# Fewer unsplit units, a gate on ScalarE alone, and stores from places of their own, in an attention and feed-forward kernel

## The chip, the cores and the metric

The kernel runs on one core of one Trainium2 chip. The metric is the device time of one execution in microseconds (us). TensorE's matmuls are called PE in the profile and its weight loads PEld; VectorE is DVE, ScalarE is ACT, GpSimd is POOL, and SyncE (SP) issues nearly all DMAs. A difference of about 0.5% is what a measurement of this kernel can tell from no change.

## The reference

Two attention steps come first and a feed-forward layer after them, for 8 batches of 576 tokens with 8 heads of 64:

```python
def sm_attn(qq, kk, vv):
    s = scale * np.matmul(qq, kk.transpose(0, 1, 3, 2))
    s = s - np.max(s, axis=-1, keepdims=True)
    a = np.exp(s)
    a = a / (np.sum(a, axis=-1, keepdims=True) + 1e-09)
    return np.matmul(a, vv)
p_packed = sm_attn(p, k, v)              # 32 packed queries over 576 keys
out = sm_attn(q, p_packed, p_packed)     # 576 queries over 32 packed keys
# x: out with its heads joined, 4608 x 512
h = x @ w_in                             # 512 -> 2048
g = h * (1.0 / (1.0 + np.exp(-1.702 * h)))
return g @ w_out                         # 2048 -> 512
```

## The kernel before

All data is fp32. A large product takes each operand as two fp32r parts, an upper part (the operand cast) and a lower part (what the cast left), and three matmuls: upper by upper, upper by lower, lower by upper. The cast is `g_upper`, `h_upper` and so on (a CAST by ScalarE at line 178 or by VectorE at line 180), the rest `g_lower` or `h_lower` (a subtraction by VectorE or GpSimd).

**Batch 0** is computed in a way of its own, while the weights still arrive: per block f of 128 hidden units and per part of the tokens, `h_mm` makes h in one of two PSUM banks (h_72 and h_73 in traces), `h_tanh` (line 729, ScalarE) takes tanh(1.702 h) from the bank, `h_gate` (line 706, VectorE) makes (tanh + 1) * h with the bank read once more, and `out_mm` (line 763) multiplies by w_out. For the exponential of the softmax (`exp1`, `exp2`) and tanh, one table of ScalarE serves; `Gelu_apprx_sigmoid` needs another table, and a switch is an ACT_TABLE_LOAD.

**Batches 1 to 7** run in rounds n = 2 to 15, two a batch, of 288 tokens each; 256 of them are worked on at once and the other 32 (the rest) are kept in DRAM until a round of their own ("over", 0) or ("over", 1) works on the rests of four batches. A round has 8 units p, one for each pair of hidden blocks. For a unit, `hp_mm` makes h of both blocks in the one two-bank PSUM tile `hh` (line 713), `hp_gelu` (line 820, ScalarE) writes the gated values to SBUF, to one of two places that take turns, and `hp_over` (line 827, a DMA that SyncE issues) stores the rest to DRAM out of that place. The next `hp_mm` can begin when `hp_gelu` has read `hh`.

The output product of a unit comes in two kinds. A unit of the set `PLAIN` is unsplit: four `plain` steps of three matmuls with 512 columns each. Any other unit is split by Winograd's scheme into seven `product` steps of three matmuls with 256 columns each. For a split unit, sums of the gated values are needed (`sums_1`, `sums_2`, `sums_3`, lines 839, 843 and 847, by VectorE or GpSimd) and the sums' upper and lower parts too (a second `g_upper` and `g_lower`), and w_out's sums are made once (`conv_1` to `conv_4`). Both kinds add up in four PSUM banks (acc_63 to acc_66 are acc[0] to acc[3]); after a round `take_1` to `take_6` join them and `keep` (line 930) stores them.

One table named `order`, written out in the kernel, holds some 3,500 steps. Each engine executes its part of the table in the table's order. An instruction that waits holds up everything behind it on its engine, and a DMA that waits for its data holds up all later DMAs of SyncE, the loads of q, k, v (`load`) and of kept weights (`win_in`, line 308) among them.

## Time and profile before

| | |
|---|---|
| median of 3 runs | 680.41 us (677.87, 680.41, 680.8) |
| profiled execution | 675.16 us |
| span of its instructions | 673.4 us |
| TensorE busy | 659.1 us, 98% of the span |
| VectorE, ScalarE, GpSimd busy | 76%, 51%, 30% of the span |
| granted TensorE clock, mean | 0.999 |

The profiled execution is one execution of its own, 0.8% under the median of the runs; 1.8 us of its time lie outside the span. "Busy" of TensorE says little about its pace, since matmuls are pipelined and their ends are modelled; starts of neighbouring matmuls tell its pace better.

### The profile page before, as it was taken

What the parts mean: (1) busy time and instruction counts of PE and PEld (TensorE: products, weight loads), DVE (VectorE), ACT (ScalarE), POOL (GpSimd) and SP (SyncE); (2) the same over time, 40 slices, a digit from 0 to 9 for tenths busy, and PEclk for the clock granted to TensorE, in tenths of its full rate; (3) what the DMA queues carried; (4) which work ended last, traced back from release to release, by engine and by line L of the source; (5) the groups of instructions that cost most, each with busy time, mean ns of one, the idle gap of its engine ahead of it and who ended that gap; (6) DMA issues with size and microseconds to landing.
All of it is one profiled execution on the core that took longest, in us unless ns stands there. A gap on an engine that the chain in (4) does not pass through costs nothing. (4 is left out here: it accounts for less than half of the span.)

```text
span 673.4 us, 15533 instructions
## 1 busy us (share of the span) xinstructions
PE 659.1 (98%) x6037; PEld 591.1 (88%) x6037; DVE 510.9 (76%) x1123; ACT 340.8 (51%) x625; POOL 201.2 (30%) x238
## 2 busy tenths in 40 slices
PE   8999999999999999999999999999999999999997
PEld 6578777897889988998899998899979998899996
DVE  4999885786988788856977558786779667856486
ACT  4887647344673557633646535662446346432332
POOL 2531123413222333223334331321434233342320
PEclk9999999999999999999999999999999999999999
DMA  8998665226535453545643536462456435210132
GB/s 339 416 373 280 220 238 189 51 68 203 172 66 158 128 163 132 132 126 177 216 142 96 125 94 188 144 198 61 129 156 199 117 95 185 70 40 9 42 110 81
DMA packets 94250, 103.10 MB, mean 153 GB/s; under 512 B 69153, under 2 KB 74209, under 8 KB 89569
## 3 DMA queue, kind: packets, MB, share of 16 engines
q1 hardware_dynamic: 94016, 101.86, 49.0%
q8 instruction: 47, 0.77, 0.5%
q10 hardware_dynamic: 160, 0.26, 0.1%
q14 instruction: 27, 0.21, 0.1%
HBM read 80.14 MB, written 21.95 MB: 152 GB/s over the span
## 5 line engine op out<-in xcount | busy, mean ns | idle before, releaser
L876 PE MATMUL acc<-at_float32r 128*128 128x256 f32 (+1 forms) x2553 | 356.8, 290 | 0.1
L876 PEld LDWEIGHTS acc<-at_float32r 128*128 128x128 f32 x2553 | 327.5, 188 | 26.8 <-issue 14.2
L713 PE MATMUL hh<-at_float32r 128*128 128x288 f32 x1344 | 207.5, 297 | 1.4 <-ACT at_float L820 0.6
L713 PEld LDWEIGHTS hh<-at_float32r 128*128 128x128 f32 x1344 | 186.0, 188 | 7.9 <-ACT at_float L820 3.1
L820 ACT ACTIVATE at_float<-hh 128x576 f32<-128x576 f32 x112 | 73.0, 652 | 173.4 <-PE hh L713 113.5
L854 DVE TENSOR_TENSOR at_float32r<-at_float,at_float32r 128x416 fp32r<-128x416 f32 (+3 forms) x188 | 124.8, 674 | 30.9 <-ACT at_float32r L178 25.7
L178 ACT CAST at_float32r<-at_float 128x416 fp32r<-128x416 f32 (+7 forms) x171 | 93.9, 561 | 79.3 <-PE acc L876 44.7
L180 DVE CAST at_float32r<-at_float 128x512 fp32r<-128x512 f32 (+5 forms) x154 | 65.6, 430 | 43.6 <-PE acc L876 29.3
L854 POOL TENSOR_TENSOR at_float32r<-at_float,at_float32r 128x512 fp32r<-128x512 f32 (+3 forms) x53 | 66.0, 1248 | 109.3 <-DVE at_float32r L180 64.8
L839 POOL TENSOR_TENSOR at_float<-at_float 128x256 f32<-128x256 f32 x34 | 26.7, 785 | 89.3 <-DVE at_float32r L854 39.5
L763 PE MATMUL acc<-at_float32r 128*128 128x512 f32 x192 | 50.2, 396 | 0.0
L612 DVE TENSOR_TENSOR at_float32r<-b,at_float32r 128x512 fp32r<-128x512 f32 (+1 forms) x64 | 42.3, 674 | 6.2 <-ACT at_float32r L178 5.9
L843 POOL TENSOR_TENSOR at_float<-at_float 128x128 f32<-128x128 f32 x42 | 21.3, 509 | 79.6 <-DVE at_float L839 61.8
L839 DVE TENSOR_TENSOR at_float<-at_float 128x256 f32<-128x256 f32 x79 | 35.5, 452 | 12.4 <-ACT at_float L820 9.5
L763 PEld LDWEIGHTS acc<-at_float32r 128*128 128x128 f32 x192 | 34.2, 188 | 9.1 <-issue 2.1
L178 ACT CAST at_float32r<-b 128x512 fp32r<-128x512 f32 (+1 forms) x52 | 28.7, 579 | 21.4 <-PE b L597 19.1
L187 ACT ACT_TABLE_LOAD x29 | 37.2, 1283 | 0.5
L597 PE MATMUL b<-at_float,at_float 64*32 64x512 f32 (+1 forms) x512 | 33.9, 586 | 0.0
L713 PEld LDWEIGHTS h<-at_float32r 128*128 128x128 f32 x192 | 27.7, 189 | 6.9 <-DVE at_float L706 1.2
L713 PE MATMUL h<-at_float32r 128*128 128x320 f32 (+1 forms) x192 | 31.1, 301 | 1.0 <-DVE at_float32r L612 0.4
L843 DVE TENSOR_TENSOR at_float<-at_float 128x128 f32<-128x128 f32 x71 | 22.8, 325 | 11.3 <-POOL at_float L839 10.4
L847 POOL TENSOR_TENSOR at_float<-at_float 128x128 f32<-128x128 f32 x36 | 19.9, 554 | 35.2 <-DVE at_float L843 26.6
(127 smaller groups left out, 560.2 us busy)
## 6 DMA issues: line engine op xcount, KB each, us to landing
at_float<-w_kept SPq DMA_DIRECT2D x24, 1024.0 KB, 5.5
at_float<-v SPq DMA_DIRECT2D x8, 1024.0 KB, 6.0
o<-at_float SPq DMA_DIRECT2D x32, 256.0 KB, 3.3
at_float<-w_out SPq DMA_DIRECT2D x16, 511.8 KB, 5.3
at_float<-q SPq DMA_DIRECT2D x14, 576.0 KB, 5.1
at_float<-w_in SPq DMA_DIRECT2D x12, 511.8 KB, 7.6
at_float<-k_last SPq DMA_DIRECT2D x8, 640.0 KB, 5.2
at_float<-pk SPq DMA_DIRECT2D x8, 576.0 KB, 5.1
```

The costliest lines, as they stand in the source:

```text
L178: nc.scalar.copy(dst, src)
L180: engine.tensor_copy(dst, src)
L187: nc.scalar.activation(small("table", 1), ident[:, :1], func)
L597: nc.tensor.matmul(banks[eo][32 * j : 32 * j + 32, columns(part)], pt(b)[rows(eo), j, :], w[rows(eo), j, columns(part)], start=True, stop= ...
L612: nc.vector.tensor_tensor(lo, t[:, at], hi.bitcast(F32), op=ALU.subtract)
L713: nc.tensor.matmul(t[:, : halves(b)[half]], m_part(fc, eo, mp)[:, fo : fo + P], a_part(b, half, ap, eo), start=(n == 0), stop=(n == len(te ...
L763: nc.tensor.matmul(acc[i], g0(f, gp)[:, i * P : (i + 1) * P], wo(f, wp), start=(start and n == 0), stop=(stop and n == 2),)
L820: nc.scalar.activation(g, h, AF.Gelu_apprx_sigmoid, scale=2.0)
L839: engine.tensor_tensor(dst, src, by, op=ALU.subtract)
L843: engine.tensor_tensor(g_raw(n, p, 6), g_raw(n, p, 5), g_raw(n, p, 1), op=ALU.add)
L854: engine.tensor_tensor(lo, src, g_range(n, p, 0, which)[0].bitcast(F32), op=ALU.subtract)
L876: nc.tensor.matmul(acc[i][:, at : at + m], lhs, rhs, start=(start and k == 0), stop=(stop and k == len(pairs) - 1),)
```

## The change

Four things change, and the order table is written anew for them.

1. `PLAIN` has 8 units instead of 15: units (2, 5), (3, 3), (3, 4), (4, 0), (4, 1), (4, 2) and (5, 0) are now split. The steps `plain` go from 60 to 32, `product` from 791 to 840, and `sums_1`, `sums_2`, `sums_3`, `g_upper`, `g_lower` get 7 more each.
2. In batch 0, blocks 0 to 3 keep `h_tanh` and `h_gate`; blocks 4 to 15 use `h_gelu`, one ScalarE instruction in place of the two (24 of 32). It uses the table of `hp_gelu`.
3. A new step `rest` copies the 32-token rests of a unit (128 x 64 values) to a place of their own, one of two that take turns by the unit's parity, and `hp_over` stores from there. There are 112 such copies, 59 on ScalarE and 53 on GpSimd.
4. In the last round, ("over", 1), the values loaded back from DRAM get six places instead of two.

```diff
-    PLAIN = {(2, 0), (2, 1), (2, 2), (2, 3), (2, 4), (2, 5), (3, 0), (3, 1), (3, 2), (3, 3), (3, 4), (4, 0), (4, 1), (4, 2), (5, 0)}
+    PLAIN = {(2, 0), (2, 1), (2, 2), (2, 3), (2, 4), (3, 0), (3, 1), (3, 2)}
...
+    def h_gelu(b, f, half):
+        nc.scalar.activation(
+            th0(f, half), st["h", f, half][:, : halves(0)[half]], AF.Gelu_apprx_sigmoid, scale=2.0
+        )
...
     def g_words(n, p, at, m):
         i = G_INDEX[n, p]
-        return words((SPARE if i == 1 else DEC + i % 2 * G_RAW) + at, m)
+        if n == ROUNDS[-1]:
+            home = (DEC, DEC + G_RAW, KQ[0], KQ[0] + 8 * P, KQ[1], KQ[1] + 8 * P)[i % 6]
+        else:
+            home = SPARE if i == 1 else DEC + i % 2 * G_RAW
+        return words(home + at, m)
...
+    def aside(n, p):
+        at = X[2 + p % 2] + S
+        return words(at, 2 * HALF_REST).rearrange("p (j r) -> p j r", j=2)
+
+    def rest(n, p, engine=nc.scalar):
+        move(engine, aside(n, p), hp_view(n, p)[0][:, :, :HALF_REST])
+
     def hp_over(n, p):
         b = n // 2
-        g = hp_view(n, p)[0][:, :, :HALF_REST]
         r = slice(n % 2 * HALF_REST, (n % 2 + 1) * HALF_REST)
         dst = over_kept[b // 4][p].rearrange("p (j t) b r -> p j t b r", t=2)
-        nc.sync.dma_start(dst[:, :, b % 4 // 2, b % 2, r], g)
+        nc.sync.dma_start(dst[:, :, b % 4 // 2, b % 2, r], aside(n, p))
...
-        (scores1_copy, 1, 1, 1, act), (h_gate, 0, 0, 1), (load_w, 18), (out_mm, 0, 0, 0),
+        (scores1_copy, 1, 1, 1, act), (h_gate, 0, 0, 1), (load_w, 19), (out_mm, 0, 0, 0),
```

What the new table does is shown at three places. The first is SyncE around the two loads of q for batch 6 (L236; the rows named "over" are stores of rests, "o" are stores of results, "w_kept" and "pk" are loads of weights and of batch 7's k). Before:

```order
L827 DMA over_95<-at_float_350 256x1x32 x2
L236 DMA at_float_104<-q 128x1152
L827 DMA over_95<-at_float_350 256x1x32
L228 DMA at_float_104<-pk 128x1152
L827 DMA over_95<-at_float_350 256x1x32
L308 DMA at_float_107<-w_kept 128x2048
L236 DMA at_float_104<-q 128x1152
L930 DMA o<-at_float_1391 128x512 x2
```

And of the change:

```order
L842 DMA over_95<-at_float_250 256x1x32
L236 DMA at_float_104<-q 128x1152
L945 DMA o<-at_float_1384 128x512
L236 DMA at_float_104<-q 128x1152
L945 DMA o<-at_float_1384 128x512
L842 DMA over_95<-at_float_272 256x1x32
L842 DMA over_95<-at_float_250 256x1x32
```

Before, the first q load is the one for the first half of the scores, and the second half's comes behind two loads of other things. Now the second half's load is issued first, a store of results of round 10 stands behind it, and the first half's load behind that store.

The second place is ScalarE in batch 0, where the exponentials of batch 1's second softmax (L666) stand among the gates of blocks 11 to 15. Before:

```order
L729 ACTIVATE at_float_350<-h_72 128x320
L178 CAST at_float32r<-at_float_350 128x512
L666 ACTIVATE at_float_133<-at_float_133 128x576
L178 COPY at_float_481<-at_float_350 128x64
L729 ACTIVATE at_float_350<-h_73 128x256
L178 CAST at_float32r<-at_float_350 128x256
L729 ACTIVATE at_float_350<-h_72 128x256
```

And of the change, where L736 is `h_gelu` and L187 the small activation that calls for a table:

```order
L736 ACTIVATE at_float_350<-h_72 128x256
L187 ACT_TABLE_LOAD
L187 ACTIVATE at_float_89<-at_float_74 128x1
L666 ACTIVATE at_float_145<-at_float_145 128x576
L178 CAST at_float32r<-at_float_350 128x256
L178 COPY at_float_483<-at_float_350 128x64
L666 ACTIVATE at_float_133<-at_float_133 128x576
L736 ACT_TABLE_LOAD
L736 ACTIVATE at_float_350<-h_73 128x256
```

The exponentials now stand between two table loads, and no gate stands between them. Over the whole kernel the table loads go from 54 to 52.

The third place is the end of VectorE's program, the takes of the last round. Before:

```order
L903 TENSOR_TENSOR at_float_350<-acc_63,at_float_1391 128x256
L906 TENSOR_TENSOR at_float_1391<-acc_64,at_float_350 128x512
L924 TENSOR_TENSOR at_float_1391<-acc_66,at_float_1391 128x256
L913 TENSOR_TENSOR at_float_1391<-acc_64,at_float_1391 128x256
L919 TENSOR_TENSOR at_float_1391<-acc_65,at_float_1391 128x512
```

And of the change:

```order
L918 TENSOR_TENSOR at_float_350<-acc_63,at_float_1384 128x256
L921 TENSOR_TENSOR at_float_1384<-acc_64,at_float_350 128x512
L928 TENSOR_TENSOR at_float_1384<-acc_64,at_float_1384 128x256
L939 TENSOR_TENSOR at_float_1384<-acc_66,at_float_1384 128x256
L934 TENSOR_TENSOR at_float_1384<-acc_65,at_float_1384 128x512
```

Two of the takes have changed places. In the table, TensorE has six `product` steps left after the last one that adds to acc[0] before the change, and eight with it.

## Rows read from the trace of the kernel before

**Rows 1.** The page's head: the span, and each engine's busy time with its share of the span and its count of instructions.

```profile
span 673.4 us, 15533 instructions
PE 659.1 (98%) x6037; PEld 591.1 (88%) x6037; DVE 510.9 (76%) x1123; ACT 340.8 (51%) x625; POOL 201.2 (30%) x238
```

**Rows 2.** Who TensorE's matmuls waited for over the whole span: us in total, times, longest us. Rows of the first 25 us are left out.

```profile
PE hh L631 <- DMA at_float<-q: 1.6, 1, 1.6
...
PE hh L631 <- ACT at_float L820: 0.8, 2, 0.5
PE hh L631 <- ACT at_float L178: 0.7, 1, 0.7
...
PE hh L713 <- ACT at_float L820: 0.6, 2, 0.4
...
PE hh L713 <- ACT at_float L178: 0.4, 2, 0.3
...
PE h L713 <- DVE at_float L706: 0.3, 1, 0.3
```

**Rows 3.** TensorE's timeline in a stretch of 512-column matmuls (L763, and L876 as `plain`): start in us, us, instruction, count.

```profile
115.37 0.84 PE L763 MATMUL acc<-at_float32r 128*128 128x512 f32 x3
116.05 1.56 PE L876 MATMUL acc<-at_float32r 128*128 128x512 f32 x6
117.45 0.85 PE L763 MATMUL acc<-at_float32r 128*128 128x512 f32 x3
118.14 0.42 PE L713 MATMUL hh<-at_float32r 128*128 128x288 f32 x2
```

**Rows 4.** TensorE's timeline at the end of the program, 256-column matmuls (`product`) alone.

```profile
638.98 29.39 PE L876 MATMUL acc<-at_float32r 128*128 128x256 f32 x246
```

**Rows 5.** Groups of instructions by line and shape over the whole span: count, busy us, mean ns of one, idle time before them. L706 is `h_gate`, L839, L843 and L847 the three sums (L843 is shown for both engines), L854 `g_lower`, L178 a cast or copy of ScalarE.

```profile
L854 DVE TENSOR_TENSOR at_float32r<-at_float,at_float32r 128x512 fp32r<-128x512 f32 x87 | 62.3, 717 | 12.6 <-ACT at_float32r L178 9.6 <-PE acc L876 0.2
...
L178 ACT CAST at_float32r<-at_float 128x512 fp32r<-128x512 f32 x61 | 37.6, 620 | 35.5 <-PE acc L876 20.8 <-DVE at_float L847 10.0 <-POOL at_float L847 3.8
...
L839 DVE TENSOR_TENSOR at_float<-at_float 128x256 f32<-128x256 f32 x79 | 35.5, 452 | 12.4 <-ACT at_float L820 9.5 <-DMA at_float<-over 1.6 <-POOL at_float32r L854 0.4
...
L843 POOL TENSOR_TENSOR at_float<-at_float 128x128 f32<-128x128 f32 x42 | 21.3, 509 | 79.6 <-DVE at_float L839 61.8 <-DVE at_float L456 9.8 <-ACT at_float32r L178 7.4
...
L843 DVE TENSOR_TENSOR at_float<-at_float 128x128 f32<-128x128 f32 x71 | 22.8, 325 | 11.3 <-POOL at_float L839 10.4
L847 DVE TENSOR_TENSOR at_float<-at_float 128x128 f32<-128x128 f32 x77 | 22.6, 296 | 6.4 <-POOL at_float L843 5.8
...
L706 DVE SCALAR_TENSOR_TENSOR at_float<-at_float,h 128x320 f32<-128x320 f32 x16 | 7.5, 481 | 1.1 <-ACT at_float L729 0.7
...
L706 DVE SCALAR_TENSOR_TENSOR at_float<-at_float,h 128x256 f32<-128x256 f32 x16 | 6.6, 412 | 1.2 <-ACT at_float L729 1.1
...
L178 ACT COPY at_float<-at_float 128x64 f32<-128x64 f32 x7 | 1.7, 246 | 0.0
```

**Rows 6.** The timelines of SyncE and of TensorE around batch 6's q loads (L236), with what TensorE waited for in brackets; the last row is the time from issue to landing of the load issued at 483.59.

```profile
475.29 0.36 SPq L236 DMA_DIRECT2D at_float<-q  x1
...
481.93 0.36 SPq L228 DMA_DIRECT2D at_float<-pk  x1
...
483.02 0.53 SPq L308 DMA_DIRECT2D at_float<-w_kept  x1
483.59 0.43 SPq L236 DMA_DIRECT2D at_float<-q  x1
...
492.99 0.72 PE L631 MATMUL hh<-at_float,at_float 64*32 64x288 f32 x16 [1.56 <-DMA at_float<-q]
...
DMA to landing us min/median/max: 9.3/9.3/9.3
```

**Rows 7.** SyncE's timeline at batch 2's q loads, the second half's issued first, and the time to landing of the one issued at 152.00.

```profile
149.81 0.56 SPq L236 DMA_DIRECT2D at_float<-q  x1
...
152.00 0.60 SPq L236 DMA_DIRECT2D at_float<-q  x1
...
DMA to landing us min/median/max: 4.9/4.9/4.9
```

**Rows 8.** The chain that ended last, its end: start us, us, what (L913 is `take_4`, L919 `take_5`).

```profile
668.41 0.34 DVE at_float L913
...
668.84 0.69 DVE at_float L919
```

**Rows 9.** ScalarE's timeline at a table switch among the later rounds: a load, and the gate that needs the table.

```profile
229.16 1.28 ACT L820 ACT_TABLE_LOAD   x1 [0.47 <-issue]
230.46 0.65 ACT L820 ACTIVATE at_float<-hh 128x576 f32<-128x576 f32 x1
```

**Rows 10.** The timelines of GpSimd and VectorE where their instructions overlap, and the durations in ns of all of VectorE's first sums (min/median/max, first and last start in us).

```profile
567.10 1.17 POOL L676 TENSOR_TENSOR at_float<-at_float,at_float 128x576 f32<-128x576 f32 x1
...
567.18 1.37 DVE L839 TENSOR_TENSOR at_float<-at_float 128x256 f32<-128x256 f32 x1 [0.43 <-POOL at_float32r L854]
...
L839 DVE TENSOR_TENSOR at_float<-at_float x79: 361/424/1370, 135.0 to 662.8; 128x256 f32<-128x256 f32 x79
```

**Rows 11.** Of ScalarE's waits (us in total, times, longest us) the one for stores of rests, and of the DMA issues those stores (count, KB each, median us to landing).

```profile
ACT at_float L820 <- DMA over<-at_float: 8.0, 3, 4.2
...
over<-at_float SPq DMA_DIRECT2D x112, 32.0 KB, 2.3
```

More of the change, by code (lines that the diff above doesn't have):

```diff
@@ new lines @@
+        (conv_whole, 3, 0, dve), (product, 2, 7, 7), (hp_mm, 3, 2, 1), (g_lower, 3, 0, 0, dve),
+        (g_upper, 3, 1, 0, act), (conv_1, 3, pool), (take_1, 2), (hp_mm, 3, 2, 0), (take_2, 2),
+        (g_lower, 3, 1, 0, pool), (take_3, 2), (hp_gelu, 3, 2), (pack, 2, (6, 7)), (take_4, 2),
+        (rest, 3, 2, pool), (take_6, 2), (pack_end, 2), (load, 'q', 2, 1), (hp_mm, 3, 3, 0),
+        (take_5, 2), (hp_over, 3, 2), (hp_mm, 3, 3, 1), (conv_2, 3), (load, 'q', 2, 0),
+        (conv_3, 3, dve), (hp_over, 3, 1), (pack_turn_mm, 2, 6), (conv_4, 3, pool),
@@ new lines @@
+        (sums_3, 5, 1, pool), (take_3, 4), (hp_mm, 5, 3, 0), (g_lower, 5, 1, 0, dve), (take_4, 4),
+        (take_6, 4), (hp_gelu, 5, 3), (pack, 3, (6, 7)), (g_upper, 5, 1, 1, dve),
+        (g_lower, 5, 1, 1, dve), (take_5, 4), (sums_1, 5, 3, pool), (pack_end, 3),
+        (load, 'q', 3, 0), (product, 5, 0, 5), (hp_mm, 5, 4, 1), (rest, 5, 3, act),
+        (rest, 5, 2, pool), (hp_over, 5, 3), (sums_2, 5, 3, dve), (sums_1, 5, 2, dve),
+        (product, 5, 0, 1), (hp_over, 5, 2), (pack_turn_mm, 3, 6), (product, 5, 0, 4),
@@ new lines @@
+        (g_upper, 7, 0, 0, act), (rest, 7, 1, pool), (g_upper, 7, 1, 0, act),
+        (g_lower, 7, 0, 0, dve), (product, 6, 7, 5), (hp_mm, 7, 2, 1), (take_2, 6), (take_3, 6),
+        (hp_gelu, 7, 2), (sums_2, 7, 1, dve), (pack, 4, (6, 7)), (sums_3, 7, 1, dve), (take_4, 6),
+        (take_6, 6), (g_lower, 7, 1, 0, dve), (pack_end, 4), (load, 'q', 4, 0), (hp_mm, 7, 3, 1),
+        (hp_over, 7, 0), (take_5, 6), (hp_mm, 7, 3, 0), (hp_over, 7, 1), (g_upper, 7, 0, 1, dve),
+        (g_lower, 7, 0, 1, dve), (keep, 6, 1), (pack_turn_mm, 4, 6), (product, 7, 0, 4),
@@ new lines @@
+        (hp_mm, 9, 2, 1), (sums_3, 9, 1, pool), (take_1, 8), (g_upper, 9, 1, 0, dve),
+        (rest, 9, 0, act), (g_lower, 9, 0, 1, dve), (hp_over, 9, 0), (product, 8, 7, 7),
+        (hp_gelu, 9, 2), (product, 8, 7, 5), (g_lower, 9, 1, 0, dve), (product, 8, 7, 3),
+        (take_2, 8), (hp_mm, 9, 3, 0), (g_upper, 9, 1, 1, act), (take_3, 8), (hp_mm, 9, 3, 1),
+        (take_4, 8), (rest, 9, 2, pool), (take_6, 8), (hp_over, 9, 2), (take_5, 8),
+        (hp_gelu, 9, 3), (pack, 5, (6, 7)), (g_lower, 9, 1, 1, dve), (sums_1, 9, 3, pool),
@@ new lines @@
+        (rest, 10, 1, act), (product, 9, 7, 7), (turn1_blocks, 6, 0), (g_upper, 10, 1, 0, act),
+        (sums_3, 10, 1, pool), (product, 9, 7, 5), (m_upper, 5, 3, 1, None, act),
+        (g_lower, 10, 1, 0, pool), (hp_mm, 10, 3, 0), (turn1_out, 6, 0, 0), (take_3, 9),
+        (product, 9, 7, 3), (hp_over, 10, 2), (take_6, 9), (product, 10, 0, 1), (take_4, 9),
+        (g_upper, 10, 1, 1, act), (load, 'v', 6, 1), (product, 10, 1, 1), (take_5, 9),
+        (hp_over, 10, 1), (product, 10, 0, 6), (g_lower, 10, 1, 1, pool), (m_lower, 5, 3, 1),
@@ new lines @@
+        (hp_gelu, 11, 2), (take_4, 10), (pack, 6, (6, 7)), (g_lower, 11, 1, 0, dve),
+        (g_upper, 11, 0, 1, act), (g_upper, 11, 1, 1, dve), (g_lower, 11, 0, 1, dve),
+        (pack_end, 6), (load, 'q', 6, 1), (hp_mm, 11, 3, 1), (take_6, 10), (rest, 11, 2, act),
+        (take_5, 10), (product, 11, 0, 6), (keep, 10, 0), (product, 11, 0, 4), (load, 'q', 6, 0),
+        (g_lower, 11, 1, 1, dve), (product, 11, 1, 4), (keep, 10, 1), (product, 11, 0, 1),
+        (sums_1, 11, 2, dve), (hp_over, 11, 1), (hp_mm, 11, 3, 0), (sums_2, 11, 2, pool),
@@ new lines @@
+        (take_4, 13), (hp_mm, 14, 3, 1), (sums_3, 14, 2, dve), (keep, 13, 0),
+        (g_lower, 14, 1, 1, pool), (take_5, 13), (product, 14, 0, 7), (hp_gelu, 14, 3),
+        (product, 14, 0, 5), (product, 14, 0, 2), (m_upper, 7, 3, 0, None, act),
+        (sums_1, 14, 3, pool), (product, 14, 1, 2), (rest, 14, 3, act), (m_lower, 7, 3, 0),
+        (product, 14, 0, 1), (hp_over, 14, 3), (product, 14, 1, 7), (keep, 13, 1),
+        (product, 14, 0, 4), (product, 14, 1, 5), (g_upper, 14, 2, 0, act), (product, 14, 1, 4),
@@ L1876 @@
+        (keep_over, ('over', 1), 0, 0), (take_5, ('over', 1)), (keep_over, ('over', 1), 1, 1, act),
+        (keep_over, ('over', 1), 1, 0),
     )
```

1784 lines of the change are left out of this document (889 added, 895 removed).

## Prediction

> **What bounds the kernel now.** I read the page's head first. TensorE is busy for 659.1 of 673.4 us, while VectorE, ScalarE and GpSimd are at 76%, 51% and 30% [rows 1]. So TensorE sets the time, unless one of the others is late for it at some place. The second view is therefore who TensorE waited for [rows 2]. After the first 25 us, which the change leaves as they are, that list is short: 1.6 us once for a load of q, and 0.8 + 0.7 + 0.6 + 0.4 + 0.3 = 2.8 us for ScalarE and VectorE, in eight pieces of at most 0.7 us. The reader is to see two things in it: work taken off the other engines can give back 2.8 us at the most, and time is otherwise won only by giving TensorE fewer columns. The third view is TensorE's pace, read from starts of neighbouring matmuls. Twelve matmuls of 512 columns fill the time from 115.37 to 118.14, 2.77 us or 0.231 us each [rows 3]. 246 matmuls of 256 columns take 29.39 us, 0.1195 us each [rows 4].
>
> **The units that are split now.** An unsplit unit is 4 steps of 3 matmuls at 512 columns: 12 x 0.231 = 2.77 us. A split one is 7 steps of 3 at 256 columns: 21 x 0.1195 = 2.51 us. Seven units win 7 x 0.26 = **1.8 us** on TensorE. All its other matmuls stay as many as they were.
>
> The price is on the other engines. At most, each of the seven units costs VectorE the three sums, 0.45 + 0.33 + 0.30 us, and a second lower part, 0.72 us, and ScalarE a second cast, 0.62 us [rows 5]: 7 x 1.80 = 12.6 us and 7 x 0.62 = 4.3 us. Against that, 24 gates of VectorE go, half at 0.481 and half at 0.412 us [rows 5], which is 10.7 us. So VectorE comes out about even, and it has a quarter of the span idle [rows 1]. I cost this at nothing. What hides it is TensorE's work on the unit before. Where that cover is gone, the next unit's g_upper and g_lower are late for its first `product`, and TensorE waits by as much.
>
> **The gate on ScalarE alone.** One activation takes the place of another on the same bank, so ScalarE's work stays; the bank is free one VectorE instruction earlier. TensorE waited 0.3 us for that instruction, L706, in all [rows 2]. That is left to the bounds. The new cost is in the order: tanh shared a table with the exponentials, and now two table loads stand around the exponentials of batch 1 within batch 0. A load takes 1.28 us and the instruction that needs it follows at once, with 0.47 us idle ahead [rows 9]. If TensorE waits for both in full, that is 2 x 1.28 = 2.6 us; if ScalarE is far enough ahead, nothing. The bank that is needed next is that of block 14, whose gate stands two behind the second load. In the table TensorE has two more `h_mm`, a chunk of M and five `out_mm` to do meanwhile, about as much work as ScalarE has there, so I take a value near the lower end, **+0.5 us**. The Trainium skill's page "ScalarE: Activation LUTs", section "What ACT_TABLE_LOAD costs", has 1283 ns for the load and a drain of about 1380 ns with it. By that, the two switches cost up to 5.3 us and the sum would end some 2.7 us higher at the worst; the trace agrees on the load and shows no more than the 0.47 us of a drain.
>
> **The copies of rests.** 59 copies on ScalarE at 0.246 us [rows 5] are 14.5 us on an engine that is 49% idle. 53 on GpSimd are not in the trace; between ScalarE's 0.246 us and the 0.509 us of GpSimd's smallest sums, of 128 x 128 values [rows 5], they are 13 to 27 us on an engine that is 70% idle. None is on the way to TensorE by itself: cost nothing, with the exceptions under the rivals. What they may win is the wait of `hp_gelu` for stores out of its place, 8.0 us in three pieces [rows 11]. Since TensorE's waits for `hp_gelu` are only 0.8 + 0.6 us altogether [rows 2], the gain is within the 2.8 us above. I leave it out of the sum.
>
> **The q loads of batch 6.** Before, the second half's load is issued at 483.59 behind loads of k (481.93) and of kept weights (483.02), lands 9.3 us later, and TensorE waits 1.6 us for it [rows 6]. In the new order it is issued first of all, right after the pack that frees its place, and has more than 10 us: **-1.6 us**. The first half's load was issued at 475.29 and TensorE did not wait for it. Now it stands behind the second half's load and behind a store of results, and that store waits for the takes of round 10 on VectorE, three of which stand there with two lower parts and a cast between them: about 3.4 us of VectorE, an estimate from the prices of such instructions [rows 5, 8]. By my count TensorE has 8.6 us of work between the start of the pack and the scores, so the load is issued some 4.8 us before it is needed. The same pair in batch 2, 2.2 us apart, had its second load land in 4.9 us [rows 7], with no store of results between. So it is late by at least 0.1 us if VectorE is in time; if it took 9.3 us as in rows 6, by 4.5. The near row is that of batch 2, and the store adds to it: I take **+0.7 us**. The bounds are 0 and 4.5.
>
> **The end.** The last matmul ends at 638.98 + 29.39 = 668.37 [rows 4], but `take_5` starts at 668.84, because `take_4` ran until then on VectorE [rows 8]. With the change eight `product` steps instead of six follow the last one into acc[0], which gives the chain of takes 2 x 3 x 0.1195 = 0.7 us more to run under matmuls. Then `take_5` waits for the last matmul alone: **-0.4 us** (bounds 0 and -0.5). The six places of the last round win nothing: in rows 4 TensorE runs without a pause there.
>
> **Sum.** -1.8 + 0.5 - 1.6 + 0.7 - 0.4 = -2.6 us. The profiled execution took 675.16 us, so 672.6, a ratio of 0.9961. The runs' median is 680.41, 0.8% above that execution, and I apply the ratio to it: **677.8 us**, 0.4% faster. That is a little less than the 0.5% that a measurement of this kernel can tell from no change.
>
> **Rivals.**
> *Given back through VectorE.* GpSimd's program grows from 243 to 331 instructions, and its work slows VectorE's: a first sum takes 424 ns in the middle and 1370 when it began 0.08 us after a GpSimd instruction of 1.17 us [rows 10]. The mean of these sums, 452 [rows 5], is 28 ns over the median. With 1.4 times the GpSimd instructions that grows by some 11 ns; over about 600 casts, sums and subtractions it is 7 us of VectorE, which would use up most of what the gates freed. TensorE feels it only where VectorE is late already. The Trainium skill's page "SBUF — State Buffer", section "Who interferes with whom", says the same more sharply: the two engines share a pair of ports under an exclusive lock, and the one that comes second blocks for the whole instruction. The trace agrees, since the 1.37 us end 0.3 us after the GpSimd instruction. If 2.6 us of this reach TensorE, the time is **680.4 us**. For it speaks that the new order also puts more split units into rounds 2 to 5; against it, that no wait in rows 2 exceeds 0.7 us there.
>
> *A wait for the store in a new place.* This one ends slower. The places of rests are two; a `rest` must wait until the store two units back has landed, 2.3 us after its issue [rows 11], and SyncE issues in order, behind waits of its own. In the closest cases of the new table only some 2.5 us of TensorE's work lie between such a store and the `rest`. A blocked `rest` on ScalarE blocks the `hp_gelu` behind it, and `hp_mm` needs `hh`. Before, the same kind of wait came to 8.0 us in three places. If as much again is exposed in full on TensorE, that is -2.6 + 8.0 = +5.4 us, **685.9 us**. The kernel is slower by over 0.5% once such waits exceed 6 us. Against it: 53 of the copies are on GpSimd, where they block no gate.
>
> *The waits vanish.* If the new order also removes the 2.8 us of rows 2, the sum is -5.4 us: **675.0 us**. For it: earlier banks in batch 0, `hp_gelu` free of stores. Against it: ScalarE gets 19 us more to do, and half of these waits are for ScalarE.
>
> **How the numbers follow.** The forecast gets 0.50, with a range of its own of 676.2 to 679.4 (the bounds of the table loads and of the late q load, short of their far ends). Given back gets 0.18, slower 0.13, vanished waits 0.19. Faster than 677.0 are the vanished waits and two fifths of the forecast: 0.39. Slower is 0.13, the same 0.48. The lower end of the range takes every gain and neither new wait: -1.8 - 1.6 - 0.4 - 2.8 = -6.6 us, which is 673.8, rounded to 674. The upper end goes past the given-back case to 682; the slower rival lies outside it.
>
> **What the profile will show.** Right: 63 more matmuls in acc, 256-column steps still near 0.12 us; no wait for q at the second half of batch 6's scores, and one under 1.5 us at the first; `take_5` starting within 0.1 us of the last matmul; a wait of `h` for ScalarE of under 1 us where the exponentials of batch 1 stand. Wrong: many waits of `hh` for ScalarE behind copies that wait for stores, waits of acc for lower parts, or a wait for q above 2 us.

## The result and the profile after

The changed kernel takes 668.64 us (median of 4 runs, 668.02 to 669.42), and the kernel before took 680.61 beside it (677.87 to 680.95): a ratio of 0.983 (95% interval 0.981 to 0.986). In a later comparison on one chip it was 668.04 against 677.67, a ratio of 0.987 (0.985 to 0.989). The kernel before spreads far more than the changed one, 674.8 to 682.5 us over all its runs, so its first median lay at the high end. Below I take 677.5 us, the median of its 111 runs beside the experiments, as its time, 668.3, between the two medians of the changed kernel, as that one's, and 9.2 us as the gain. The forecast was 677.8 with a range from 674.0: far too little.

The profiled execution of the changed kernel took 668.02 us. First the page's head, which answers to [rows 1]:

```profile
span 666.2 us, 15795 instructions
PE 655.2 (98%) x6100; PEld 592.6 (89%) x6100; DVE 501.2 (75%) x1087; ACT 358.9 (54%) x697; POOL 229.7 (34%) x326
```

The span is 7.2 us shorter than in [rows 1]. TensorE has 63 matmuls more. Next, everything that TensorE's matmuls waited for after the first 25 us, which answers to [rows 2]:

```profile
PE hh L713 <- DVE at_float L180: 0.5, 1, 0.5
PE hh L631 <- DMA at_float<-q: 0.4, 1, 0.4
PE b L597 <- DVE at_float32r L612: 0.3, 1, 0.3
PE acc L768 <- DVE at_float32r L300: 0.3, 1, 0.3
PE acc L891 <- DVE at_float32r L869: 0.2, 1, 0.2
PE acc L768 <- POOL at_float32r L763: 0.2, 1, 0.2
```

In the kernel before this list came to 4.6 us in seven rows, of which [rows 2] shows six. Now it is 1.9. Not one wait of `hh` for ScalarE is left. I also worked out, from the starts of all matmuls, how much longer each took to the next start than is usual for its pair of shapes. By that the two traces differ by 1.9 us of columns and 5.2 us of waiting. On balance all of the 5.2 come after 188 us of the span. The list shows 2.7 of them. The rest are slips too short for it, and the part of a listed wait that lies under the modelled end of the matmul before.

ScalarE's waits for stores of rests, which answer to [rows 11], are now those of the copies alone; no gate (L829) waits for one:

```profile
ACT at_float L178 <- DMA over<-at_float: 3.0, 4, 1.3
```

SyncE and TensorE around batch 6's q loads, which answers to [rows 6] (the first load is for the second half, the second for the first half, whose scores start at 474.35):

```profile
466.52 0.35 SPq L236 DMA_DIRECT2D at_float<-q  x1
467.60 0.36 SPq L945 DMA_DIRECT2D o<-at_float  x1
468.01 0.42 SPq L236 DMA_DIRECT2D at_float<-q  x1
...
474.35 0.72 PE L631 MATMUL hh<-at_float,at_float 64*32 64x288 f32 x16 [0.39 <-DMA at_float<-q]
484.66 0.72 PE L631 MATMUL hh<-at_float,at_float 64*32 64x288 f32 x16
```

Three groups that the forecast priced, which answer to [rows 5]: the first sums and the copies of rests on either engine.

```profile
L854 DVE TENSOR_TENSOR at_float<-at_float 128x256 f32<-128x256 f32 x90 | 41.1, 458 | 27.7 <-ACT at_float L829 15.8 <-POOL at_float32r L869 9.4 <-DMA at_float<-over 1.2
...
L178 ACT COPY at_float<-at_float 128x64 f32<-128x64 f32 x68 | 16.0, 242 | 3.6 <-DMA over<-at_float 3.0
...
L180 POOL COPY at_float<-at_float 128x64 f32<-128x64 f32 x53 | 15.2, 291 | 61.6 <-ACT at_float L829 45.6 <-ACT at_float32r L178 6.6 <-issue 6.2
```

ScalarE's timeline in batch 0 where the exponentials (L666) now stand between two table loads:

```profile
86.21 0.38 ACT L736 ACTIVATE at_float<-h 128x256 f32<-128x256 f32 x1 [1.74 <-PE h L713]
86.61 1.28 ACT L187 ACT_TABLE_LOAD   x1
...
89.03 0.68 ACT L666 ACTIVATE at_float<-at_float 128x576 f32<-128x576 f32 x1
89.73 1.28 ACT L736 ACT_TABLE_LOAD   x1
91.03 0.38 ACT L736 ACTIVATE at_float<-h 128x256 f32<-128x256 f32 x1
```

TensorE waits for neither. And the chain's end, which answers to [rows 8], with SyncE's last stores from its timeline:

```profile
654.91 6.42 PE acc L891 x54
...
661.35 0.69 DVE at_float L934
...
660.92 2.02 SPq L950 DMA_DIRECT2D o<-at_float  x2
```

### The profile page after: what moved, and what is told of

Read it like the earlier page. It is cut to its first block, busy times and chain, and to the rows that moved or that the text cites. A ratio compares the mean times of both kernels' runs of the same rounds, so it can differ in the third digit from the quotient of the medians.

```text
span 666.2 us, 15795 instructions
## 1 busy us (share of the span) xinstructions
PE 655.2 (98%) x6100; PEld 592.6 (89%) x6100; DVE 501.2 (75%) x1087; ACT 358.9 (54%) x697; POOL 229.7 (34%) x326
## 4 chain that ended last, share of the span: by engine, by line
PE 85%; DVE 5%; DMA 5%; ACT 1%; issue 1%; SPq 1%; POOL 0%; DVEq 0%; ACTq 0%; POOLq 0%
PE acc L891 46%; PE hh L713 25%; PE acc L768 5%; PE b L597 4%; PE h L713 3%; DMA at_float<-w_in 2%; DMA over<-at_float 1%; PE hh L631 1%; DMA at_float<-w_out 1%; PE b L525 1%; DMA at_float<-q 1%; PE hh L376 1%; ACT at_float32r L178 1%; DVE at_float32r L869 1%; DVE at_float32r L612 0%
## 5 line engine op out<-in xcount | busy, mean ns | idle before, releaser
L829 ACT ACTIVATE at_float<-hh 128x576 f32<-128x576 f32 x112 | 73.0, 652 | 161.3 <-PE hh L713 107.6
L869 DVE TENSOR_TENSOR at_float32r<-at_float,at_float32r 128x512 fp32r<-128x512 f32 (+3 forms) x187 | 125.0, 678 | 34.9 <-ACT at_float32r L178 28.5
L178 ACT CAST at_float32r<-at_float 128x512 fp32r<-128x512 f32 (+7 forms) x183 | 102.6, 574 | 69.4 <-PE acc L891 45.8
L869 POOL TENSOR_TENSOR at_float32r<-at_float,at_float32r 128x416 fp32r<-128x416 f32 (+3 forms) x61 | 76.3, 1254 | 78.7 <-ACT at_float32r L178 40.0
L180 DVE CAST at_float32r<-at_float 128x512 fp32r<-128x512 f32 (+4 forms) x149 | 60.9, 415 | 35.2 <-PE acc L891 20.9
L854 DVE TENSOR_TENSOR at_float<-at_float 128x256 f32<-128x256 f32 x90 | 41.1, 458 | 27.7 <-ACT at_float L829 15.8
L862 POOL TENSOR_TENSOR at_float<-at_float 128x128 f32<-128x128 f32 x65 | 35.8, 554 | 70.8 <-DVE at_float L858 60.6
L858 POOL TENSOR_TENSOR at_float<-at_float 128x128 f32<-128x128 f32 x50 | 26.1, 521 | 64.9 <-DVE at_float L854 55.5
L854 POOL TENSOR_TENSOR at_float<-at_float 128x256 f32<-128x256 f32 x30 | 22.9, 764 | 50.2 <-ACT at_float L829 28.6
L178 ACT CAST at_float32r<-b 128x512 fp32r<-128x512 f32 (+1 forms) x54 | 30.0, 578 | 16.4 <-PE b L597 16.4
L180 POOL COPY at_float<-at_float 128x64 f32<-128x64 f32 x53 | 15.2, 291 | 61.6 <-ACT at_float L829 45.6
L713 PE MATMUL h<-at_float32r 128*128 128x256 f32 (+1 forms) x192 | 30.7, 301 | 0.7 <-DVE at_float32r L612 0.4
```

The lines of the kernel that those rows point to most:

```text
L178: nc.scalar.copy(dst, src)
L180: engine.tensor_copy(dst, src)
L713: nc.tensor.matmul(t[:, : halves(b)[half]], m_part(fc, eo, mp)[:, fo : fo + P], a_part(b, half, ap, eo), start=(n == 0), stop=(n == len(te ...
L829: nc.scalar.activation(g, h, AF.Gelu_apprx_sigmoid, scale=2.0)
L854: engine.tensor_tensor(dst, src, by, op=ALU.subtract)
L862: engine.tensor_tensor(g_raw(n, p, 7), g_raw(n, p, 3), g_raw(n, p, 6), op=ALU.subtract)
```

## The experiments

Runs named b_ edit the kernel before, runs named a_ edit the changed kernel. Ratios are to the kernel before, run on the same chip in turns.

**The kernel before again (b_again).** No edit.

> The kernel before, unchanged. Its timed runs lie at 677.9 to 681.0 us, its first profiled execution at 675.2. Theory S (stores): the difference between executions is time that TensorE waits for gated activations held up by stores of rests, so a further profile with a longer time shows more than the 8.0 us of ScalarE's waits for stores, and more of TensorE's waits for the gated activation than 1.4 us. Theory P (the place where it ran): the waits are those of the first profile, and the time differs elsewhere or everywhere alike. Time under both: 680.6, ratio 1.000.

678.51 us, 1.002 (0.999 to 1.004). Its profiled execution took 677.0 us, 1.8 more than the one that the forecast was read from. The waits for stores and the waits of TensorE in it (lines are one higher):

```profile
ACT at_float L821 <- DMA over<-at_float: 13.3, 6, 4.2
...
PE hh L377 <- ACT at_float L821: 1.9, 1, 1.9
PE hh L632 <- ACT at_float L821: 1.3, 3, 0.6
...
PE hh L714 <- ACT at_float L821: 0.6, 2, 0.4
```

The same kernel waits 13.3 us for stores here and 8.0 in [rows 11], and TensorE's waits for gates are 3.8 us against 0.8 + 0.6 in [rows 2]. One profile is one draw, and the forecast had a good one.

**Three single edits in the kernel before (b_rest, b_q, b_fewer).** The copies of rests, each right ahead of its store; batch 6's second q load right behind the first; eight of the 512-column matmuls left out in the seven units (a lower product is missing there), which takes as much off TensorE as splitting them.

```diff
+    order = [s for step in order
+        for s in (((rest, *step[1:], pool if step[1:] in ON_POOL else act), step) if step[0] is hp_over else (step,))]
...
+    order = [step for step in order if step != (load, "q", 6, 1)]
+    order.insert(order.index((load, "q", 6, 0)) + 1, (load, "q", 6, 1))
...
-        add_up(n, 2 if t else 3, 0, DM, [(hi, wo(f, 0)), (hi, wo(f, 1)), (lo, wo(f, 0))])
+        add_up(n, 2 if t else 3, 0, DM, [(hi, wo(f, 0)), (hi, wo(f, 1)), *last])
```

> The kernel before with one part of the change alone: each rest is copied to a place of its own right ahead of its store in the order, on the same engine as in the changed kernel, and stored from there; everything else in the old order. Theory S: most of the gain that is not in fewer columns comes with it, -4 to -7 us, about 675. Theory O (the new order as a whole removes many small waits): without the new order the copies alone win at most the waits for stores of the first profile, -1 to -1.5 us, about 679.3, or nothing because the copies hold up ScalarE.

> The kernel before with one load moved: the second half of q for batch 6 is issued right behind the first half. If the 1.6 us wait of the profile is there in every execution and nothing else takes its place: -1.6 us, about 679.0. If the q load then stands behind the stores and the later loads come late instead: 0.

> The kernel before without 8 of TensorE's 512-column matmuls in the seven units that the change splits (the product of lower part and upper part in one step of each unit, and in two steps of unit (2, 5), is left out): 8 x 0.231 = 1.85 us less work for TensorE, as much as splitting the units saves, at no cost elsewhere. If columns are time in those rounds: -1.85 us, about 678.8. If the other engines set the pace there and TensorE only waits more: less than -0.8 us, above 679.8.

b_rest: 676.43 us, 0.998 (0.997 to 1.000). b_q: 675.65, 0.9975 (0.995 to 1.000). b_fewer: 676.04, 0.997 (0.995 to 0.999). Against 677.54 beside them that is 1.1, 1.9 and 1.5 us. So the copies alone win what Theory O said, and not Theory S's 4 to 7 us. In b_rest no gate waits for a store any more, but a part of the gain went into TensorE's wait for q, 2.5 us where [rows 2] has 1.6. First that wait, then the page's row of the granted clock in 40 slices of the span (in tenths, 9 is 90% or more):

```profile
PE hh L631 <- DMA at_float<-q: 2.5, 1, 2.5
...
PEclk9999999999999999999999999999989999999999
```

The slice with the 8 lies right behind the wait. The scores that waited start at 493.31, and from 494.1 to 497.5 us the granted clock is 0.50, which is its level of 1.2 GHz; before and after it is 1.00. From these scores to the second `hp_mm` behind them TensorE takes 5.0 us, where the kernel before takes 3.5 for the same matmuls. So this late q cost the profiled execution 0.9 us of waiting more and about 1.6 us by the clock. That the wait brings the fall is argued: in b_again the clock stayed at 1.00 behind a wait of 1.9 us. Of b_rest's timed runs four have a mean clock of 0.997 or less. Five others have a median of 675.4 us, 1.7 under the runs of the kernel before with a clock of 0.998 or more (677.1).

**The three together (b_all).**

> The kernel before with three single edits together, each of which was run alone: copies of rests right ahead of their stores (0.9984), the second load of q for batch 6 right behind the first (0.9975), eight matmuls of 512 columns left out (0.9974; a part of the output product is missing). If their gains add up, the ratio is 0.9933 (673.0 us where the kernel before takes 677.5). If they hide one another's waits, it is 0.996 or more. If each takes away what kept the others from counting, it is under 0.991, and then little is left for the order as a whole.

671.75 us (671.5 to 671.94), 0.9915 (0.990 to 0.993), so 5.9 us faster, where the single ones add up to 4.5. That lies between gains that add up (0.993) and gains that need each other (under 0.991). With q in time, what b_rest lost to it is back: no wait for q and no fall of the clock before the last matmul stand in b_all's trace. The spread has shrunk from 7 us to 0.4 in four runs. By its columns this kernel is level with the changed one; the changed kernel still has some 3.5 us over it.

**The changed kernel again, and without the copies (a_again, a_store).** In a_store the stores read the gated values' own place, at the place where the copy stood:

```diff
+    order = [(hp_over, *step[1:3]) if step[0] is rest else step for step in order if step[0] is not hp_over]
```

> The changed kernel, run again beside the kernel before on the same chip. If the first comparison caught the kernel before at its slow end (it read 680.4 us then and 677.5 in the later runs), the ratio comes out nearer 0.987 than 0.983. If the two move together from chip to chip, it stays at 0.983. Either way the spread of the changed kernel's own times should be under 1.5 us, as in its first runs, against 6 us for the kernel before.

> The changed kernel with the copies of rests taken away: each store reads the gated values where they lie, and is issued at the place where the copy stood. Theory R (the gain that the three priced parts leave open is the gates' waits for stores): the gates wait again, some 10 us in all, TensorE waits for them, and 3 to 5 us come back, a ratio of 0.988 to 0.991. Rival O (the new order as a whole took TensorE's waits away, and copies are one way among others): the waits of the gates come back but TensorE has work meanwhile, under 1.5 us comes back, a ratio under 0.986.

a_again: 668.04 us, 0.987 (0.985 to 0.989), spread 667.25 to 670.53. a_store: 678.14, 1.001 (0.998 to 1.003): all of the gain is gone, 10.1 us, more than either theory said. The table is the one that was written for the copies. ScalarE's and TensorE's waits over the whole of a_store, and one place of it, ScalarE's row first:

```profile
ACT at_float L829 <- DMA over<-at_float: 13.1, 5, 4.9
...
ACT L829 <- DMA over<-at_float: 5.9, 4, 2.2
...
PE hh L713 <- ACT at_float L829: 4.6, 5, 1.9
```

```profile
308.22 0.65 ACT L829 ACTIVATE at_float<-hh 128x576 f32<-128x576 f32 x1 [3.02 <-DMA over<-at_float]
...
306.47 1.23 PE L892 MATMUL acc<-at_float32r 128*128 128x256 f32 x9
308.93 0.72 PE L631 MATMUL hh<-at_float,at_float 64*32 64x288 f32 x16 [1.23 <-ACT at_float L829]
```

The gate waits 3.0 us for a store to land, TensorE has nine matmuls to do meanwhile, and then it stands 1.2 us. Worked out from the starts of all matmuls as above, TensorE waits 9.2 us longer than in a_again, and 9.1 of that come after 105 us. A part is the clock again: behind the longest wait for a gate, which ends at 452.55, it is at 0.50 from 452.7 to 456.1 us, which costs about half of these 3.4 us. So in the new order the gain hangs on the copies. How much they bring by themselves this does not show.

**The gate part (b_gate, a_gate, a_gate2, a_gate3).** b_gate has it alone in the old order, for 18 of the 24 gates. The others are the changed kernel with tanh and VectorE's gate back in all blocks: a_gate as the table stands, a_gate2 with 44 steps of batch 0 back on the engines of the kernel before, a_gate3 with VectorE's gates up to two steps later.

```diff
+            (h_gelu, *step[1:]) if step[0] is h_tanh and step[2:] in ALONE else step,
...
+        for s in (((h_tanh, *step[1:]), (h_gate, *step[1:])) if step[0] is h_gelu else (step,))
...
+    order = [(*s[:-1], ENGINES[s[:-1]]) if s[:-1] in ENGINES else s for s in order]
...
+    for gate_step in [x for x in order if x[0] is h_gate and x[2] >= 4]:
+        order = later(order, gate_step)
```

> The kernel before with the gate part alone, in the old order: 18 of the 32 gates of batch 0 are one activation of ScalarE, their VectorE instructions gone (some 8 us of VectorE), with two table loads more. Theory G (the gate part gives time by itself, since VectorE is 87 to 93% busy in batch 0): 1 to 3 us faster, a ratio of 0.996 to 0.9985. Rival (TensorE did not wait for VectorE there, so that nothing is won and the two loads may cost up to 2.6 us): 0.999 to 1.004.

> The changed kernel with the gate of batch 0 as before: tanh by ScalarE and the product by VectorE in all sixteen blocks, and no table loads for the exponentials there. Theory G (VectorE's 10.7 us of gates held up its work in batch 0 and behind it): 2 to 4 us come back, a ratio of 0.987 to 0.990. Rival (batch 0 is bound by TensorE and its loads either way): within 1 us of the changed kernel, a ratio of 0.982 to 0.985, or a little less, since the table loads are gone.

> The changed kernel with the gate of batch 0 as before, and with 44 casts, subtractions and copies of batch 0 back on the engines that did them before. Putting the gate back alone cost 8.7 us, all of it between 20 and 105 us of the span. If that was VectorE being too full there (its gates had made room for casts that came over from ScalarE), TensorE gets most of it back: a loss of 0 to 4 us against the changed kernel, a ratio of 0.986 to 0.992. If it was the place of the gates in the order, the loss stays at 7 to 9 us, 0.996 to 1.000.

> The changed kernel with the gate of batch 0 as before, as in the earlier run that took 676.7 us, but with each of VectorE's gates two of its instructions later, so that it does not stand waiting for the tanh. If the place of the gates was the cost, 3 to 6 us of the 8.7 come back, a ratio of 0.990 to 0.995. If VectorE's load was, it stays at 0.997 to 1.000.

b_gate: 679.32 us, 1.003 (1.002 to 1.005), so 2.1 us slower than the kernel before; the seven of its 12 runs with a mean clock of 0.998 or more are 1.3 slower than such runs of the kernel before. a_gate: 676.68, 0.9985 (0.997 to 1.000). a_gate2: 677.57, 1.000 (0.998 to 1.001). a_gate3: 678.14, 1.000 (0.999 to 1.002). These three lose 8.6 to 10.1 us against the changed kernel. The start of batch 2's first scores in the changed kernel and in a_gate, from TensorE's timeline, shows where:

```profile
104.86 0.66 PE L376 MATMUL b<-at_float 64*32 64x256 f32 x16
```

```profile
113.83 0.66 PE L376 MATMUL b<-at_float 64*32 64x256 f32 x16
```

9.0 us are lost by then, out of 10.7 between the two spans. In a_gate TensorE's longest waits up to there are for VectorE:

```profile
PE b L597 <- DVE at_float32r L612: 1.4, 1, 1.4
PE h L713 <- DVE at_float32r L612: 1.3, 3, 0.7
```

The new order of batch 0 needs the gate part. The part itself wins nothing: alone it costs 1.3 to 2.1 us. Both the engines of the casts and the place of the gates fell as causes of a_gate's loss (a_gate2, a_gate3 are no faster). By its expectation a_gate3 leaves VectorE's load standing, and TensorE's waits above are for VectorE, but no run took work off VectorE there: between 25 and 104 us it is busy for 68.0 us in a_gate and 67.9 in a_gate2. What in batch 0 makes the loss stays open.

**What the order adds to the three edits (b_swap, b_swap2, b_light, b_both, a_dve).** In b_all the waits that the changed kernel does not have stand mostly between 190 and 320 us. First the largest of b_all's rows of TensorE's waits in that stretch, then ScalarE's and TensorE's timelines at the largest:

```profile
PE hh L713 <- ACT at_float L820: 1.1, 2, 0.9
```

```profile
192.99 1.28 ACT L187 ACT_TABLE_LOAD   x1
...
194.40 0.57 ACT L178 CAST at_float32r<-b 128x512 fp32r<-128x512 f32 x1
194.86 0.25 ACT L178 COPY at_float<-at_float 128x64 f32<-128x64 f32 x1
195.01 0.65 ACT L820 ACTIVATE at_float<-hh 128x576 f32<-128x576 f32 x1
...
192.74 0.94 PE L713 MATMUL hh<-at_float32r 128*128 128x288 f32 x6
193.51 1.31 PE L882 MATMUL acc<-at_float32r 128*128 128x512 f32 x5
195.71 1.88 PE L713 MATMUL hh<-at_float32r 128*128 128x288 f32 x12 [0.88 <-ACT at_float L820]
```

The gate of `hh` stands behind a table load, a cast and a copy, while TensorE has five matmuls left to do. In the changed kernel the gate comes right behind the load, and TensorE has 21 smaller matmuls there:

```profile
192.43 1.28 ACT L187 ACT_TABLE_LOAD   x1
...
193.83 0.64 ACT L829 ACTIVATE at_float<-hh 128x576 f32<-128x576 f32 x1
...
192.48 2.67 PE L891 MATMUL acc<-at_float32r 128*128 128x256 f32 x21
```

Busy times by stretch (PE, PEld, DVE, ACT, POOL), of b_all and then of the changed kernel:

```profile
105.00:180.00 75.00, 74.66 (x617) 62.11 (x617) 55.40 (x109) 39.39 (x73) 26.73 (x31) 1.00 0.47 134
180.00:235.00 55.00, 53.75 (x503) 49.06 (x495) 45.13 (x96) 30.15 (x56) 17.20 (x23) 1.00 0.45 127
235.00:310.00 75.00, 74.12 (x744) 68.29 (x731) 57.84 (x129) 40.11 (x73) 24.38 (x38) 1.00 0.46 133
```

```profile
105.00:180.00 75.00, 74.93 (x638) 64.55 (x629) 64.63 (x127) 40.58 (x74) 29.55 (x38) 1.00 0.46 133
180.00:235.00 55.00, 55.00 (x556) 52.22 (x549) 39.17 (x89) 33.18 (x67) 24.60 (x34) 1.00 0.44 123
235.00:310.00 75.00, 75.00 (x746) 69.80 (x746) 53.38 (x118) 42.91 (x78) 28.44 (x42) 1.00 0.51 154
```

VectorE does 9.2 us more between 105 and 180 us now, and 10.4 less from there to 310. A part of that is forced by the split units: w_out's sums must be ready before the first split unit that uses them, and VectorE's `conv_whole` (L335) is 12 times instead of 5 in the first stretch. So there were two things to try in b_all: other work for TensorE ahead of a late `hh` (b_swap: up to three ready `product` or `plain` steps moved ahead at eleven places; b_swap2: at ten), and a lighter VectorE (b_light: 15 second lower parts left out). b_both has ten moves and the lighter VectorE. a_dve is the reverse of b_light, 14 idle sums in the changed kernel.

```diff
+    for step, many in (((scores2_mm, 2, 0, (4, 5)), 2), ((hp_mm, 4, 4, 0), 3), ...):
+        order = ahead(order, step, many)
...
+    LOWER = [x for x in order if x[0] is g_lower and x[1] in (4, 5, 6, 7) and x[3] == 1 and x[4] is dve]
+    order = [x for x in order if x not in LOWER[:15]]
...
+        nc.vector.tensor_reduce(ff(0)[:, 0:1], wo(14, 0).bitcast(F32), axis=AX.X, op=ALU.add)
```

> The three single edits together as before (0.9915), and at eleven places up to three steps of the output product that are ready are moved on TensorE ahead of a step that waited for hh there (4.3 us of such waits in its trace, at 157.8 to 491.5 us). Theory O (what the new order adds to the three edits is that TensorE has other work where it waited): 3 to 4 us faster than the three edits, a ratio of 0.9855 to 0.9875, as the changed kernel. Rival (the gates are late for other reasons and the waits come back one step on): 0.990 to 0.9925.

> The three single edits together (671.75 us, 0.9915), and 15 of VectorE's subtractions of rounds 4 to 6 left out (the second lower part of those units, so that old values are multiplied in its place): some 10.5 us less of VectorE between 190 and 275 us of the span, TensorE's work the same. Theory V (VectorE held the gates and casts up there): 1.5 to 3.5 us faster than the three edits, a ratio of 0.986 to 0.989. Rival (the waits come from ScalarE's own order, its table loads and the gates behind them): 0.990 to 0.992.

> The changed kernel with 14 idle sums over 512 values on VectorE, one behind every second gate of rounds 4 to 7 (184 to 305 us of the span), about 0.7 us each, so that VectorE has some 10 us more to do there, as in the kernel before. Theory V: 1.5 to 3.5 us slower than the changed kernel, a ratio of 0.989 to 0.992. Rival (VectorE has room there and only the order counts): within 0.7 us of it, 0.986 to 0.988.

> As the run with the moved steps of TensorE (671.94 us), without the first of the eleven moves, after which a wait of 1.1 us stood at 165 us. That wait should go: 670.9 to 671.3 us, a ratio of 0.9900 to 0.9908. If something else takes its place, 671.8 as before.

> The ten moves and the 15 subtractions of VectorE left out (their products use old values). If the two gains only add up, 1.1 us less than without the subtractions left out: some 670.0 us, a ratio of 0.989. If they need each other (TensorE has other work, and VectorE is ready for it), 668.3 to 669.2, a ratio of 0.9863 to 0.9876: then order and load together are the rest of the gain. If the waits that the moves made are ScalarE's, 670.6 or more.

b_swap: 671.94 us, 0.992 (0.991 to 0.994), nothing won; in its trace the moves took some waits away and made others, the largest of 1.1 us at 165 us. b_swap2, without that move: 670.97, 0.990 (0.988 to 0.993). b_light: 670.62, 0.990 (0.987 to 0.992). a_dve: 669.73, 0.988 (0.986 to 0.991), 1.7 us over a_again (by the starts of matmuls 1.0 in the stretch itself, 0.9 at 493 to 507 us). b_both: 669.70, 0.988 (0.986 to 0.991).

So of the 3.5 us that the changed kernel has over b_all, TensorE's order gives 0.8 and a lighter VectorE 1.1 to 1.3, and the two simply add. Theory O fell in size: b_swap lies in its rival's range, and 0.8 us are left of 3 to 4. Theory V was right in kind and too high: b_light falls between it and its rival, a_dve at its lower end. The last 1.4 us are not separated; ScalarE's order, as in the rows at 193 us, is what is left, argued and not run alone. These medians lie 0.8 to 1.3 us apart with spreads of 0.2 to 1.7 us, on chips where the medians of the kernel before agree within 0.5 us; the ratios' intervals are wider, since the kernel before spreads. The starts of all matmuls say the same: against b_all TensorE waits 1.1 us less in b_swap2, 1.4 in b_light and 2.8 in b_both.

**More work for TensorE (a_more).** The changed kernel with 42 more 256-column matmuls (a lower term is added twice in three units of each round).

```diff
+        again = [(lo, bhi)] if isinstance(n, int) and p in (5, 6, 7) and k == 1 else []
+        add_up(n, i, at, 256, [(hi, bhi), (hi, blo), *again, (lo, bhi)])
```

> The changed kernel with 42 matmuls of 256 columns more, one in each of three units of every round (a term of the output product is added twice there). If TensorE has no slack anywhere in those rounds, it is 42 x 0.1195 = 5.0 us slower than the changed kernel, a ratio of 0.993 to 0.995 to the kernel before. If a part of its time is waiting that extra work would fill, it is 2 to 4 us slower.

672.05 us, 0.993 (0.991 to 0.995): 4.0 us over a_again, of 5.0 for the matmuls. TensorE's work is time nearly everywhere.

**Two places in the last round (a_two).** The loads of the last round come early in the new table, so with two places values are overwritten before their casts: units of that round are made from other units' values.

```diff
-        if n == ROUNDS[-1]:
+        if False:
```

> The changed kernel with the values of the last round in two places instead of six. The forecast put the six places at nothing, since TensorE ran without a pause there before the change: then it is within 0.5 us of the changed kernel, 0.986 to 0.988. Rival: in the new order the loads of the last round are issued too early for two places and wait for them, and TensorE with them: 1 to 5 us slower, 0.989 to 0.995.

680.64 us, 1.005 (1.003 to 1.007), 12.6 us over a_again. The largest of TensorE's waits from 600 us on, and the busy times of that stretch, the granted clock third from the end:

```profile
PE acc L891 <- DVE at_float32r L869: 3.2, 5, 1.7
...
600.00:675.00 75.00, 67.11 (x498) 63.86 (x497) 42.96 (x91) 20.09 (x41) 22.02 (x31) 0.95 0.19 52
```

All waits there come to 5.3 us. Behind the one of 1.7 us the clock is at 0.50 from 636.3 to 643.1 us, which costs about half of these 6.8 us more. The new order needs the six places as it needs the gate part. That they win time by themselves this does not show.

## Why the prediction was wrong

The forecast's sum was -2.6 us. Between the two profiled spans it was -7.2, between the medians some -9.2.

- **Columns, -1.8: right.** The starts of all matmuls give 1.9, b_fewer 1.5.
- **q of batch 6, -1.6 + 0.7: right in its steps.** No wait at the second half, 0.39 us at the first, so -1.2. The load issued at 468.01 landed 6.2 us later, between the two bounds; TensorE was ready for it 5.9 us after the issue, not 4.8 (8.6 less 3.4 would be 5.2). b_q measured 1.9 for the edit alone in the old order.
- **Table loads, +0.5: mis-sized, 0 in the trace.** ScalarE was far enough ahead in the new order. In the old order a load did cost: in b_gate's trace TensorE waits 1.0 us at 46.4 us for the first of the new gates, which stands behind a table load, and not at all for the loads at the exponentials. So b_gate's loss is no measure of this term. The Trainium skill's page "ScalarE: Activation LUTs", section "What ACT_TABLE_LOAD costs", has a drain of about 1380 ns with a load of 1283. The trace agrees on the load alone: the second one starts 0.02 us after the exponential's 89.03 + 0.68, and the gate 0.02 us after the load.
- **The end, -0.4: given back.** `take_5` starts 0.03 us after TensorE's last piece in the chain, as foreseen. But SyncE issues the second of its two last stores 0.4 us after `take_5` ends, where it was 0.1 before (its row of 2.02 us holds both, and the wait between them), and from the last matmul to the end of the span it is 4.9 us, against 5.0.
- **The ceiling of 2.8 us, and with it stores of rests at 0: the step that failed.** "Since TensorE's waits for `hp_gelu` are only 0.8 + 0.6 us altogether, the gain is within the 2.8 us above. I leave it out of the sum." Columns and q are 3.1 to 3.4 of the 9.2 us, so the rest is about 6, twice the ceiling (4.0 between the two spans). The bound was read from one execution, and b_again has 3.8 us of waits for gates. A wait that the list does not show was taken as none: half of the 5.2 us that went does not show in it. And what a wait costs by a lower clock behind it was left out, 1.6 us in b_rest's profile. The copies alone win 1.1 us; beyond q and the columns the three edits together win some 2.5.
- **VectorE's work, "I cost this at nothing".** In total it did come out even, 501.2 us against 510.9. Its place in time counted: with 10.5 us less of it between 190 and 275 us b_light wins 1.1.
- **"Time is otherwise won only by giving TensorE fewer columns."** This fell with the ceiling: 5.2 of the 7.2 us between the spans came without fewer columns. What a_more shows is the other side, that added columns cost 4.0 of 5.0 us.
- **The base.** The ratio was applied to 680.41, the median of three runs, where the kernel's time is nearer 677.5. That added some 3 us to the miss: from 677.5 the forecast would have been 674.9, and the result is 668.3.
- **The rivals.** "The waits vanish" was the right one: every row of ScalarE's and VectorE's waits in [rows 2] is gone, and new ones come to 1.5 us. Against it stood that half of these waits are for ScalarE; by [rows 2] it is 2.5 of the 2.8 us. Its -5.4 us fell short by what the list does not show. "Given back through VectorE" fell: the first sums take 458 ns, 452 in [rows 5], with 326 instructions on GpSimd (238 before in [rows 1], where the forecast has 243 and 331). "A wait for the store in a new place" occurs, 3.0 us in four pieces on ScalarE's copies, and TensorE has no wait from it; GpSimd's copies take 291 ns, within their bounds.

The account of the 9.2 us: 5.8 by the three edits that the forecast had named, together; 2.0 by TensorE's order and VectorE's load, mostly between 190 and 320 us; some 1.4 not separated. Which part looks largest depends on the execution: by the starts of matmuls b_all's profile waits 1.4 us less than the one that the forecast was read from, 3.2 less than b_again's, and some 3.7 more than the changed kernel's. The gate part and the six places have no gain of their own in this account. They are what the new order stands on.

## What to carry to other kernels

A list of waits from one execution can fall well short of what waits cost: look at a second execution, and at the spread of the runs, before a gain is bounded by it. Look at the granted clock behind a long wait of TensorE as well, since the wait may not be all that is lost. A wait for a DMA that an engine meets in some executions only can be worth removing even if that engine looks far from the path. Where several parts come with one new order, undoing a part measures what the order leans on, and doing it alone in the old order measures what it brings; the two can differ in sign, as for the gate (2.1 us slower alone, 8.6 slower undone).

## What the runs showed that I had not expected

How long the same stores keep the gates waiting differs between executions by more than half: 8.0, 13.3, 11.0, 8.9 and 8.8 us in five executions of kernels with those waits in the old order (before, b_again, b_q, b_fewer, b_gate). The spread of the runs shrinks with such waits, from 7.7 us in the kernel before (674.8 to 682.5) to 2.3 in nine of b_rest's ten runs and 0.4 in b_all; the tenth run of b_rest took 2237 us, which nothing here explains. The changed kernel spreads over 3.3, so stores are not all of it. The clock is a part of it: 26 of the 111 runs of the kernel before have a mean granted clock of 0.997 or less and a median of 679.3 us, the other 85 a median of 677.1, and none of the changed kernel's eight runs is under 0.998. In the profiles of b_rest, b_gate and a_store it fell to 1.2 GHz for 3.4 us behind a wait of TensorE of 1.9 to 2.5 us, in a_two for 6.8 us.
